# Tails of four heads in one product, two more transposes by DMA, and two MoE pieces begun on half their tokens

## Chip, core and metric

The kernel runs on one core of a Trainium2 chip. Its time is the device time of one execution in microseconds (us), and a kernel's time is the median over several executions.

## The reference

A forgetting attention, whose output is the input of a two-layer MoE block with a SiLU gate (one expert, no routing). 8 batches, 8 heads, 576 positions, head size 64; 4608 tokens of width 512, inner width 2048.

```python
scores = scale * np.matmul(q, k.transpose(0, 1, 3, 2))
cum = np.cumsum(np.log(np.clip(f, 0.0001, 1.0)), axis=-1)
scores = np.where(causal, -1e9, scores + cum[..., :, None] - cum[..., None, :])
attn = softmax(scores)
x = np.matmul(attn, v).transpose(0, 2, 1, 3).reshape(B * S, H * D)
h = x @ w_in
out = (h * (1.0 / (1.0 + np.exp(-h)))) @ w_out
```

The row part of the decay cancels in the softmax; the column part, exp(-cum), is multiplied into v and into a 65th column of ones beside it, so that one product gives both the weighted sum and its divisor.

## The kernel before

The order of the instructions of every engine is the order in which the Python code emits them. Three streams are woven together by hand: loads and conversions (queues of SP and POOL), attention, and MoE pieces that `fill` (through `slot`) emits between steps of the attention so that TensorE (PE) never has to stand.

**Positions.** 576 positions of a sequence are cut into a head of 128 (block 0), a rest of 384 and a tail of 64. All heads of the sequence blocks 0 are computed first, batch by batch (`turn0`, `scores0`, `out0`, `back0`): scores, exp on ScalarE (ACT), product with v, division on VectorE (DVE), and a transpose on PE whose copy (L391, ACT or DVE) writes the MoE input `x`. The first MoE group holds the heads of batches 0 to 3, 512 tokens; batches 4 and 5, then 6 and 7 follow as groups of 256.

**Rest and tails.** The main loop (`for m in range(NQ)`, 16 rounds) takes two units n = 2m and 2m + 1; a unit is two heads of a batch, and a batch is four units. `prepare` casts q and k for unit n + 2 on POOL (L400, L404), has SP transpose them by DMA (L428, `qkT`), and has SP load q, k for unit n + 4 (L158), the tails (L168) and v (L179); POOL multiplies v by its weights (L414). All of SP's transfers stand in one queue in the emitted order, and so do POOL's casts, multiplies and output stores (L592). `scores` makes the scores in three chunks (L460), their exp (L464, and L476 for the tails' `ut`), and DVE masks them (L469, and L483 for `ut`). `attend` multiplies by v into the PSUM tile `dn` (L507: 18 matmuls of 65 columns), and the tails of the unit's two heads follow into a seventh column group of the same tile (L516: 10 matmuls of 65 columns). There the left operand is 128 wide: 64 positions of one head beside 64 zeros, so that two heads accumulate into the two halves of the partitions. The zeros stand in the middle of `ut`, which has three parts (head, zeros, head); POOL writes them once with four memsets (L735). DVE then takes the reciprocal of the 65th column (L524) and multiplies (L525) into `xr`.

**Back.** `back(m - 1)` is emitted in round m, between the scores of the two units and ahead of the second `prepare`. For rounds with `BY_DMA[m]` (m from 4 to 14) SP transposes `xr` into `x` (L539) and the tails into `xt` (L543) by DMA; for the others PE transposes it in 7 matmuls (L549) and DVE copies it in two instructions (L552, L555). Each round has four `slot`s. A rest group becomes `ready` for MoE with the end of the next slot after its second `back`, and one slot later where that goes by DMA.

**MoE.** `m1_chunk(g, fc)` makes one of 16 pieces of the inner width for group g: 4 matmuls (L568) into a PSUM tile `hp`, tanh on ACT (L576) and the gate on DVE (L577), which writes `gt`. `m2_part` makes a quarter of the second layer for 128 tokens (L613, tile `po`, 4 matmuls); ACT copies the sum (L623) and POOL stores it (L592). `step` chooses between the two and goes on with whichever layer lags.

**Buffers.** The PSUM pool `pbig` has four buffers for `hp`, `po`, `dn`, `tx` and the rest; `sc` has two of its own (`psc`). A tile's buffer comes free when its last reader has finished, for `hp` the gate on DVE, for `dn` the multiply L525. `after` (L200) is a small transfer at the head of SP's main-loop loads that waits until half of w_out has landed.

Of the kernel before, what the change touches and what calls it, by code (L numbers as in the profile page):

```python
# [12 lines left out]
P = 128  # L13
# [5 lines left out]
def kernel(  # L19
# [62 lines left out]
    kT0 = [const.tile([P, NP, P], BF16, name=f"kT0_{b}") for b in range(B)]  # L82
    v0 = [const.tile([P, H, D + 1], BF16, name=f"v0_{b}") for b in range(B)]
    vps = [const.tile([P, NM, H, D + 1], BF16, name=f"vp_{i}") for i in range(2)]
    uts = [const.tile([P, NM + 1, 3, ST], BF16, name=f"ut_{i}") for i in range(4)]
    vfs = [const.tile([P, H, D + 1], FP32, name=f"vf_{i}") for i in range(4)]


# [356 lines left out]
    def scores(n, c):  # L445
        b, p = divmod(n, NP)
        if c == 0:
            us[n] = upool.tile([P, 2, UW], BF16, name="u", tag="u")
        u, ut = us[n], uts[n % 4]
        t = qkT[n]  # L450
        sc = psc.tile([P, 2, SM], FP32, name="sc", tag="sc")
        for kb, q0, q1, o in CHUNKS[c]:
            for i in range(2):
                r = slice(i * D, (i + 1) * D)
                if kb == 0:
                    kt = kT0[b][r, p, :]
                else:
                    k0 = RB if kb == NM else kb * P + RB
                    kt = t[r, k0 : k0 + P]
                nc.tensor.matmul(  # L460
                    sc[:, i, o : o + q1 - q0], lhsT=kt, rhs=t[r, q0:q1], start=True, stop=True
                )
        w = SM if c < 2 else T0
        nc.scalar.activation(  # L464
            out=u[:, :, c * SM : c * SM + w], in_=sc[:, :, 0:w], func=ACT.Exp, scale=scale
        )
        if c == 0:
            x = u[:, :, 0:RB].rearrange("p i (a t) -> p i a t", t=P)
            nc.vector.tensor_tensor(  # L469
                out=x,  # L470
                in0=x,
                in1=tri[:, None, None, :].to_broadcast([P, 2, NR, P]),
                op=ALU.mult,
            )
        if c == 2:
            nc.scalar.activation(  # L476
                out=ut[:, :, 0:3:2, :].rearrange("p k i t -> p i k t"),
                in_=sc[:, :, T0 : T0 + (NM + 1) * ST].rearrange("p i (k t) -> p i k t", t=ST),
                func=ACT.Exp,
                scale=scale,  # L480
            )
            x = ut[:, NM, 0:3:2, :]
            nc.vector.tensor_tensor(  # L483
                out=x, in0=x, in1=trit[:, None, :].to_broadcast([P, 2, ST]), op=ALU.mult
            )

    NGR = 2 * NR + 1

    BY_DMA = [2 * 2 <= m < NQ - 1 for m in range(NQ)]

    def attend(n):
        b, p = divmod(n, NP)
        if p % 2 == 0:
            xqs[n // 2] = xqp.tile([P, NGR, 2, D], BF16, name="xr", tag="xr", bufs=3)
        xq = xqs[n // 2]
        u, ut = us.pop(n), uts[n % 4]
        dn = pbig.tile([P, NGR, D + 1], FP32, name="dn", tag="big")

        def vals(kb, i):
            h = head(p, i)  # L500
            return v0[b][:, h, :] if kb == 0 else vbf[b][:, kb - 1, h, :]

        for i in range(2):
            for c in range(1, NM):
                for kb in range(c + 1):
                    o = AT[c, kb]
                    nc.tensor.matmul(  # L507
                        dn[:, i * NR + c - 1, :],
                        lhsT=u[:, i, o : o + P],
                        rhs=vals(kb, i),  # L510
                        start=(kb == 0),
                        stop=(kb == c),
                    )
        for i in range(2):
            for kb in range(NM + 1):
                nc.tensor.matmul(  # L516
                    dn[:, NGR - 1, :],
                    lhsT=ut[:, kb, i : i + 2, :].rearrange("p i t -> p (i t)"),
                    rhs=vals(kb, i),
                    start=(i == 0 and kb == 0),  # L520
                    stop=(i == 1 and kb == NM),
                )
        rec = recp.tile([P, NGR], FP32, name="rec", tag="rec")
        nc.vector.reciprocal(out=rec[:, :], in_=dn[:, :, D])  # L524
        nc.vector.tensor_tensor(  # L525
            out=xq[:, :, p % 2, :],
            in0=dn[:, :, 0:D],
            in1=rec[:, :, None].to_broadcast([P, NGR, D]),
            op=ALU.mult,
        )  # L530

    def back(m):
        b, c0 = m // 2, m % 2 * 2
# [24 lines left out]

    gts: dict[int, bass.AP] = {}

    def m1_chunk(g, fc):
        w = GW[g]
        if fc == 0:
            gts[g] = gpool.tile([P, NFC, w], BF16, name="gt", tag="gt")
        gt = gts[g]
        hp = pbig.tile([P, w], FP32, name="hp", tag="big")
        for cc in range(NCC):
            nc.tensor.matmul(  # L568
                hp[:, :],
                lhsT=w_in_bf[:, cc, fc * P : (fc + 1) * P],  # L570
                rhs=xcols(g, cc),
                start=(cc == 0),
                stop=(cc == NCC - 1),
            )
        th = tpool.tile([P, w], BF16, name="th", tag="th")
        nc.scalar.activation(out=th[:, :], in_=hp[:, :], func=ACT.Tanh, scale=0.5)  # L576
        nc.vector.scalar_tensor_tensor(  # L577
            out=gt[:, fc, :],
            in0=th[:, :],
            scalar=1.0,  # L580
            in1=hp[:, :],
            op0=ALU.add,
            op1=ALU.mult,
        )
# [142 lines left out]
    back0(1, on_act)  # L727
    out0(3, 1)
    back0(2, on_act)
    back0(3, on_act, on_dve)  # L730
    ready.add(0)
    nc.gpsimd.memset(trit[0:ST, :], 0.0)
    make_upper_triangular(nc, trit[ST:P, :], val=1.0, diag=True)
    for t in uts:
        nc.gpsimd.memset(t[:, :, 1, :], 0.0)  # L735
    for t in vps:
        nc.gpsimd.memset(t[0:ST, NR, :, :], 0.0)
    load_w_out(0)
# [84 lines left out]
    def slot(us_, first=0):  # L823
        n = len(stores)
        fill(us_, first)
        store(n)
        for x in pending:
            x[0] -= 1
        while pending and pending[0][0] == 0:
            ready.update(pending.pop(0)[1])  # L830

    for m in range(NQ):
        n = 2 * m
        piece = 1.7 if m < 2 else 2.4
        scores(n, 0)
        scores(n, 1)
        prepare(n)
        slot(piece, 2)
        if m > 0:
            back(m - 1)  # L840
            if m % 2 == 0:
                b = m // 2 - 1
                pending.append([1 + BY_DMA[m - 1], [REST_OF[b]] + ([TAILS_OF[b][0]] if b == NM - 1 else [])])
        scores(n, 2)
        scores(n + 1, 0)
        prepare(n + 1)
        slot(piece, 2)
        scores(n + 1, 1)
        scores(n + 1, 2)
        slot(piece, 2)  # L850
        attend(n)
        attend(n + 1)
        slot(min(3.5, max(0.8, behind() - LAG)) if m > 1 else 0.8, 1)
    back(NQ - 1)
    ready.update([REST_OF[B - 1], TAILS_OF[B - 1][0]])
# [36 lines left out]
```

The softmax here doesn't subtract the row's maximum and nothing guards it: scores larger than these inputs give would overflow.

## Time and profile before

| what | value |
|---|---|
| median of 6 runs | 347.32 us (345.23 to 348.28) |
| the profiled execution's own time | 348.45 us |
| its span, first to last instruction | 346.6 us |
| PE sc (L460) | 128-column matmuls x384, 64-column x256 and others |
| PE dn L507 / L516 | 576 / 320 matmuls of 65 columns |
| PE tx L549 | 35 matmuls, in 5 of 16 rounds |
| SP transposes | qkT x32, x x11, xt x11 |
| DVE L524 / L525 | 32 each, 203 / 624 ns |
| DVE L577, 384 columns | 128, 553 ns |
| ACT L576, 384 columns | 128, 504 ns |
| POOL memset of ut, L735 | 4, 1.28 us in all from 21.84 us |

A row of the groups gives engine, line, operation, the names and sizes of what is written and read, the number of instructions and their mean time. PE's durations overlap, because matmuls are pipelined: the time that one costs is the time from its start to the next one's start, so the text uses start-to-start times. A wait is put down to the engine and line that ended last before it. In the slices, a digit is a tenth of 8.67 us.

### The profile page before, as it was taken

Reading aid. Unit: us, or ns where it says so; the run is one execution under the profiler, and the core shown is the slowest. Engines: PE = TensorE matmul, PEld = TensorE weight load, DVE = VectorE, ACT = ScalarE, POOL = GpSimd, SP = SyncE. Lnnn points to the kernel's source line nnn. Section 1 sums busy time; section 2 is a strip of 40 time slices with the busy share of each in tenths; the row PEclk is TensorE's granted clock in tenths of the full one; section 3 lists DMA queues with packets and bytes.
Section 4 is the critical chain, followed back from the end, with each engine's and each line's share of the span. In section 5 each row is a group of like instructions: output and inputs, shape, how many; then the busy total and the mean of one; then the engine's idle time right before and its main releaser. Section 6 shows DMA issues by size and latency. Waiting matters only on the chain.

```text
span 346.6 us, 8892 instructions
## 1 busy us (share of the span) xinstructions
PE 335.8 (97%) x3567; PEld 199.2 (57%) x3567; DVE 185.8 (54%) x389; ACT 218.0 (63%) x401; POOL 129.2 (37%) x227
## 2 busy tenths in 40 slices
PE   8999999969998999999999999999999999999995
PEld 3654556647655566466565665656655565555654
DVE  4766645455668466457646654646645453535330
ACT  5866654866685857768759576685775934545341
POOL 8996224823518264236218126234420000010011
PEclk9999999999999999999999999999999999999999
DMA  8999989999689999899889989989832100010103
GB/s 154 197 185 220 200 160 150 220 210 185 164 177 208 187 201 158 170 210 167 154 193 187 159 154 220 158 191 188 170 91 56 35 32 30 32 46 32 46 36 87
DMA packets 141497, 50.44 MB, mean 146 GB/s; under 512 B 132368, under 2 KB 138768, under 8 KB 141456
## 3 DMA queue, kind: packets, MB, share of 16 engines
q1 hardware_dynamic: 131440, 32.70, 52.4%
q0 software_dynamic: 9856, 17.04, 21.1%
q8 instruction: 28, 0.46, 0.6%
q10 hardware_dynamic: 160, 0.13, 0.1%
q14 instruction: 13, 0.11, 0.1%
HBM read 36.85 MB, written 9.44 MB: 134 GB/s over the span
## 4 chain that ended last, share of the span: by engine, by line
PE 73%; DMA 11%; POOL 5%; SPq 4%; issue 3%; ACT 1%; DVE 1%; POOLq 0%
PE po L613 30%; PE hp L568 28%; PE sc L460 6%; PE dn L507 4%; DMA w_out_bf<-in_moe_w_out_dram 3%; DMA vf<-in_v_dram 3%; PE dn L516 2%; DMA qktf<-in_k_dram 2%; SPq L158 2%; DMA qf<-in_q_dram 2%; PE wm L232 1%; SPq L168 1%; DMA qkT<-qkb 1%; POOL v L341 1%; POOL w_in_bf L190 1%
## 5 line engine op out<-in xcount | busy, mean ns | idle before, releaser
L576 ACT ACTIVATE th<-hp 128x384 bf16<-128x384 f32 (+2 forms) x208 | 96.0, 478 | 90.9 <-PE hp L568 88.6
L577 DVE SCALAR_TENSOR_TENSOR gt<-th,hp 128x384 bf16<-128x384 bf16 (+2 forms) x208 | 106.0, 522 | 79.7 <-ACT th L576 76.1
L613 PE MATMUL po<-w_out_bf,gt 128*128 128x512 bf16 (+1 forms) x592 | 144.7, 374 | 0.0
L568 PE MATMUL hp<-x,w_in_bf 128*128 128x384 bf16 (+2 forms) x704 | 128.9, 322 | 0.2
L568 PEld LDWEIGHTS <-w_in_bf 128*128 128x128 bf16 x832 | 78.5, 98 | 55.2 <-issue 2.2
L464 ACT ACTIVATE u<-sc 128x1024 bf16<-128x1024 f32 (+1 forms) x96 | 75.2, 823 | 13.1 <-PE sc L460 13.0
L613 PEld LDWEIGHTS <-gt 128*128 128x128 bf16 x592 | 54.6, 98 | 49.7 <-issue 2.1
L592 POOL DMA_DIRECT2D out_dram<-osb x38 | 21.0, 552 | 130.2 <-ACT osb L623 83.0
L414 POOL TENSOR_TENSOR vp<-vf,w_bf 128x520 bf16<-128x520 f32 (+1 forms) x32 | 34.0, 1065 | 32.0 <-DMA vf<-in_v_dram 24.1
L469 DVE TENSOR_TENSOR u<-u,tri 128x768 bf16<-128x768 bf16 x32 | 22.2, 693 | 20.2 <-ACT u L464 20.1
L400 POOL CAST qkb<-qf 128x384 bf16<-128x384 f32 x32 | 17.6, 551 | 36.2 <-DMA qf<-in_q_dram 35.8
L483 DVE TENSOR_TENSOR ut<-ut,trit 128x128 bf16<-128x128 bf16 x32 | 12.0, 376 | 34.8 <-ACT ut L476 34.8
L623 ACT ACTIVATE osb<-po 128x512 f32<-128x512 f32 (+1 forms) x37 | 22.0, 596 | 12.4 <-PE po L613 12.3
L460 PE MATMUL sc<-qkT 64*128 64x128 bf16 (+1 forms) x640 | 26.5, 207 | 3.1 <-DMA qkT<-qkb 3.1
L460 PEld LDWEIGHTS <-qkT 64*128 64x128 bf16 x640 | 18.2, 95 | 14.1 <-issue 9.1
L476 ACT ACTIVATE ut<-sc 128x640 bf16<-128x640 f32 x32 | 23.4, 730 | 0.0
L507 PEld LDWEIGHTS <-u 128*128 128x128 bf16 x576 | 20.7, 98 | 4.1 <-issue 1.8
L507 PE MATMUL dn<-vp,u 128*128 128x65 bf16 x384 | 21.8, 194 | 0.0
L507 PE MATMUL dn<-v,u 128*128 128x65 bf16 x192 | 19.8, 194 | 1.6 <-DVE gt L577 1.6
L525 DVE TENSOR_TENSOR xr<-dn,rec 128x448 bf16<-128x448 f32 x32 | 20.0, 624 | 1.1
L400 POOL CAST qkb<-kf 128x384 bf16<-128x384 f32 x32 | 17.4, 542 | 6.5 <-DMA kf<-in_k_dram 6.5
L568 PE MATMUL hp<-xt,w_in_bf 128*128 128x256 bf16 x128 | 18.2, 273 | 0.3 <-DVE gt L577 0.2
(68 smaller groups left out, 205.3 us busy)
## 6 DMA issues: line engine op xcount, KB each, us to landing
out_dram<-osb POOLq DMA_DIRECT2D x32, 256.0 KB, 3.1
vf<-in_v_dram SPq DMA_DIRECT2D x26, 256.0 KB, 5.1
qf<-in_q_dram SPq DMA_DIRECT2D x64, 96.0 KB, 2.9
kf<-in_k_dram SPq DMA_DIRECT2D x64, 96.0 KB, 2.8
w_in_bf<-in_moe_w_in_dram POOLq DMA_DIRECT2D x4, 512.0 KB, 6.9
w_out_bf<-in_moe_w_out_dram POOLq DMA_DIRECT2D x4, 512.0 KB, 9.6
vf<-in_v_dram POOLq DMA_DIRECT2D x6, 256.0 KB, 10.2
qkb<-in_q_dram POOLq DMA_DIRECT2D x8, 128.0 KB, 5.2
```

Source lines behind the costliest of these rows:

```text
L400: nc.gpsimd.tensor_copy(out=t2[:, c0 : c0 + NR, :].rearrange("p c x -> p (c x)"), in_=t[:, :, :, :].rearrange("p c h d -> p (c h d)"),)
L414: nc.gpsimd.tensor_tensor(out=vbf[b][r, c, :, :], in0=vst[b][c][r, :, :], in1=w_bf[r, c + 1, b * H : (b + 1) * H, None].to_broadcast([n, H ...
L460: nc.tensor.matmul(sc[:, i, o : o + q1 - q0], lhsT=kt, rhs=t[r, q0:q1], start=True, stop=True)
L464: nc.scalar.activation(out=u[:, :, c * SM : c * SM + w], in_=sc[:, :, 0:w], func=ACT.Exp, scale=scale)
L469: nc.vector.tensor_tensor(out=x, in0=x, in1=tri[:, None, None, :].to_broadcast([P, 2, NR, P]), op=ALU.mult,)
L476: nc.scalar.activation(out=ut[:, :, 0:3:2, :].rearrange("p k i t -> p i k t"), in_=sc[:, :, T0 : T0 + (NM + 1) * ST].rearrange("p i (k t) ...
L507: nc.tensor.matmul(dn[:, i * NR + c - 1, :], lhsT=u[:, i, o : o + P], rhs=vals(kb, i), start=(kb == 0), stop=(kb == c),)
L568: nc.tensor.matmul(hp[:, :], lhsT=w_in_bf[:, cc, fc * P : (fc + 1) * P], rhs=xcols(g, cc), start=(cc == 0), stop=(cc == NCC - 1),)
L576: nc.scalar.activation(out=th[:, :], in_=hp[:, :], func=ACT.Tanh, scale=0.5)
L577: nc.vector.scalar_tensor_tensor(out=gt[:, fc, :], in0=th[:, :], scalar=1.0, in1=hp[:, :], op0=ALU.add, op1=ALU.mult,)
L613: nc.tensor.matmul(po[:, :], lhsT=gt[:, fc, tb * P : (tb + 1) * P], rhs=w_out_bf[:, fc, m0:m1], start=(fc == 0), stop=(fc == NFC - 1),)
L623: nc.scalar.activation(out=osb[:, :], in_=po[:, :], func=ACT.Copy, scale=0.5)
```

## The change

Four edits stand in the diff. `ut` loses its zeros: it has two parts, and the four memsets go. `attend` leaves the tails out; a new `attend_tails(m)` is emitted once per round after both units' `attend`, takes a PSUM tile `dt` from `pbig`, and multiplies the tails of two heads (128 columns, no zeros) by the values of both heads at once (130 columns): 10 matmuls for a round instead of 20, of whose result half is used. DVE takes one reciprocal and two multiplies of 64 partitions for it. `BY_DMA` begins at m = 2 instead of 4, which also makes batch 1's rest group ready one slot later, so that in round 4 two products of the second layer change places with two pieces of the first on the two sides of the attention. And `m1_begin` makes the first 256 columns (batches 0 and 1) of the first two MoE pieces, one ahead of the fourth batch's transposes and one behind them; `m1_chunk` then makes the other 256 columns of these two. SP, POOL and ACT otherwise keep their order (on ACT one tanh moves behind a copy in round 4).

```diff
@@ -82,7 +82,7 @@
     kT0 = [const.tile([P, NP, P], BF16, name=f"kT0_{b}") for b in range(B)]
     v0 = [const.tile([P, H, D + 1], BF16, name=f"v0_{b}") for b in range(B)]
     vps = [const.tile([P, NM, H, D + 1], BF16, name=f"vp_{i}") for i in range(2)]
-    uts = [const.tile([P, NM + 1, 3, ST], BF16, name=f"ut_{i}") for i in range(4)]
+    uts = [const.tile([P, NM + 1, 2, ST], BF16, name=f"ut_{i}") for i in range(4)]
     vfs = [const.tile([P, H, D + 1], FP32, name=f"vf_{i}") for i in range(4)]
 
 
@@ -474,27 +474,27 @@
             )
         if c == 2:
             nc.scalar.activation(
-                out=ut[:, :, 0:3:2, :].rearrange("p k i t -> p i k t"),
+                out=ut[:, :, :, :].rearrange("p k i t -> p i k t"),
                 in_=sc[:, :, T0 : T0 + (NM + 1) * ST].rearrange("p i (k t) -> p i k t", t=ST),
                 func=ACT.Exp,
                 scale=scale,
             )
-            x = ut[:, NM, 0:3:2, :]
+            x = ut[:, NM, :, :]
             nc.vector.tensor_tensor(
                 out=x, in0=x, in1=trit[:, None, :].to_broadcast([P, 2, ST]), op=ALU.mult
             )
 
     NGR = 2 * NR + 1
 
-    BY_DMA = [2 * 2 <= m < NQ - 1 for m in range(NQ)]
+    BY_DMA = [2 <= m < NQ - 1 for m in range(NQ)]
 
     def attend(n):
         b, p = divmod(n, NP)
         if p % 2 == 0:
             xqs[n // 2] = xqp.tile([P, NGR, 2, D], BF16, name="xr", tag="xr", bufs=3)
         xq = xqs[n // 2]
-        u, ut = us.pop(n), uts[n % 4]
-        dn = pbig.tile([P, NGR, D + 1], FP32, name="dn", tag="big")
+        u = us.pop(n)
+        dn = pbig.tile([P, 2 * NR, D + 1], FP32, name="dn", tag="big")
 
         def vals(kb, i):
             h = head(p, i)
@@ -511,23 +511,42 @@
                         start=(kb == 0),
                         stop=(kb == c),
                     )
-        for i in range(2):
-            for kb in range(NM + 1):
-                nc.tensor.matmul(
-                    dn[:, NGR - 1, :],
-                    lhsT=ut[:, kb, i : i + 2, :].rearrange("p i t -> p (i t)"),
-                    rhs=vals(kb, i),
-                    start=(i == 0 and kb == 0),
-                    stop=(i == 1 and kb == NM),
-                )
-        rec = recp.tile([P, NGR], FP32, name="rec", tag="rec")
+        rec = recp.tile([P, 2 * NR], FP32, name="rec", tag="rec")
         nc.vector.reciprocal(out=rec[:, :], in_=dn[:, :, D])
         nc.vector.tensor_tensor(
-            out=xq[:, :, p % 2, :],
+            out=xq[:, 0 : 2 * NR, p % 2, :],
             in0=dn[:, :, 0:D],
-            in1=rec[:, :, None].to_broadcast([P, NGR, D]),
+            in1=rec[:, :, None].to_broadcast([P, 2 * NR, D]),
             op=ALU.mult,
         )
+
+    def attend_tails(m):
+
+
+        b, h0 = m // 2, m % 2 * 4
+        xq = xqs[m]
+        dt = pbig.tile([P, 2, 2, D + 1], FP32, name="dt", tag="big")
+        for w in range(2):
+            ut = uts[(2 * m + w) % 4]
+            for kb in range(NM + 1):
+                vals = v0[b] if kb == 0 else vbf[b][:, kb - 1, :, :]
+                nc.tensor.matmul(
+                    dt[:, w, :, :],
+                    lhsT=ut[:, kb, :, :].rearrange("p i t -> p (i t)"),
+                    rhs=vals[:, h0 + w : h0 + 4 : 2, :],
+                    start=(kb == 0),
+                    stop=(kb == NM),
+                )
+        rec = recp.tile([P, 2, 2], FP32, name="rect", tag="rect")
+        nc.vector.reciprocal(out=rec[:, :, :], in_=dt[:, :, :, D])
+        for i in range(2):
+            r = slice(i * ST, (i + 1) * ST)
+            nc.vector.tensor_tensor(
+                out=xq[r, 2 * NR, :, :],
+                in0=dt[r, :, i, 0:D],
+                in1=rec[r, :, i, None].to_broadcast([ST, 2, D]),
+                op=ALU.mult,
+            )
 
     def back(m):
         b, c0 = m // 2, m % 2 * 2
@@ -558,17 +577,36 @@
 
     gts: dict[int, bass.AP] = {}
 
+    begun: dict[int, bass.AP] = {}
+
+    def m1_begin(fc):
+
+        w = GW[0] // 2
+        hp = pbig.tile([P, GW[0]], FP32, name="hp", tag="big")
+        for cc in range(NCC):
+            nc.tensor.matmul(
+                hp[:, 0:w],
+                lhsT=w_in_bf[:, cc, fc * P : (fc + 1) * P],
+                rhs=xg(0)[:, cc, 0:w],
+                start=(cc == 0),
+                stop=(cc == NCC - 1),
+            )
+        begun[fc] = hp
+
     def m1_chunk(g, fc):
         w = GW[g]
         if fc == 0:
             gts[g] = gpool.tile([P, NFC, w], BF16, name="gt", tag="gt")
         gt = gts[g]
-        hp = pbig.tile([P, w], FP32, name="hp", tag="big")
+        if g == 0 and fc in begun:
+            hp, c0 = begun.pop(fc), w // 2
+        else:
+            hp, c0 = pbig.tile([P, w], FP32, name="hp", tag="big"), 0
         for cc in range(NCC):
             nc.tensor.matmul(
-                hp[:, :],
+                hp[:, c0:w],
                 lhsT=w_in_bf[:, cc, fc * P : (fc + 1) * P],
-                rhs=xcols(g, cc),
+                rhs=xcols(g, cc) if c0 == 0 else xg(g)[:, cc, c0:w],
                 start=(cc == 0),
                 stop=(cc == NCC - 1),
             )
@@ -727,12 +765,12 @@
     back0(1, on_act)
     out0(3, 1)
     back0(2, on_act)
+    m1_begin(0)
     back0(3, on_act, on_dve)
+    m1_begin(1)
     ready.add(0)
     nc.gpsimd.memset(trit[0:ST, :], 0.0)
     make_upper_triangular(nc, trit[ST:P, :], val=1.0, diag=True)
-    for t in uts:
-        nc.gpsimd.memset(t[:, :, 1, :], 0.0)
     for t in vps:
         nc.gpsimd.memset(t[0:ST, NR, :, :], 0.0)
     load_w_out(0)
@@ -850,6 +888,7 @@
         slot(piece, 2)
         attend(n)
         attend(n + 1)
+        attend_tails(m)
         slot(min(3.5, max(0.8, behind() - LAG)) if m > 1 else 0.8, 1)
     back(NQ - 1)
     ready.update([REST_OF[B - 1], TAILS_OF[B - 1][0]])
```

## The prediction

> **What bounds the kernel now.** I read the page first.
>
> ```profile
> span 346.6 us, 8892 instructions
> ...
> PE 335.8 (97%) x3567; PEld 199.2 (57%) x3567; DVE 185.8 (54%) x389; ACT 218.0 (63%) x401; POOL 129.2 (37%) x227
> ...
> PEclk9999999999999999999999999999999999999999
> DMA  8999989999689999899889989989832100010103
> ```
>
> TensorE is busy 97% of the span at an undiminished clock, so its time is the sum of its instructions' start-to-start times plus its few waits. The DMA engines are as full until slice 28 (about 250 us). The waits of PE (in total, times, longest) say where these two meet:
>
> ```profile
> PE sc L460 <- DMA qkT<-qkb: 3.1, 2, 2.6
> PE dn L507 <- DVE gt L577: 1.6, 1, 1.6
> ```
>
> Then the chain that ended last, in order of time (start, us, what), in the stretch of the first of these waits:
>
> ```profile
> 75.09 1.22 SPq L428
> ...
> 78.60 4.68 DMA vf<-in_v_dram
> 83.28 3.77 DMA qkT<-qkb
> 87.04 0.05 issue
> 87.09 0.40 PE sc L460 x8
> 87.49 1.41 PE hp L568 x12
> ```
>
> Up to 87.09 us the chain runs through SP's queue and its loads, and PE stands waiting twice (2.6 us before 75.97, 0.4 before 87.09) for transposed q and k. From 87 us on the chain is PE. So **what PE saves before 87 us is waited away**, and what it saves or loses after it counts. I number units n (two heads) and pairs of units m as the code does; 87.09 is the scores of unit 5.
>
> **Begun pieces.** They issue 8 matmuls of 256 columns ahead and 8 in place of 8 of 512. Rows: 256 columns 109 ns start to start, 512 columns 216, so the columns cost the same. They fill holes: between the third and fourth batches' transposes PE stands from 16.62 to 17.09, then 17.21 to 17.42 and 17.54 to 17.84, 0.98 us. ScalarE's copy of batch 1 ends at 16.81; piece 0 runs 16.86 to 17.30, the fourth batch's transposes go 0.2 late, piece 1 runs 17.53 to 17.97, the second halves 18.03 to 18.90. The third piece starts at 18.90 instead of 17.84 + 8 x 0.216 = 19.57: 0.67 us ahead. In the built program the fifth piece is still the first to need a buffer back (the first piece's). Worth at the end: **0**, since the 2.6 us wait for unit 3's qkT takes it.
>
> **Zeros no longer written.** Four memsets of POOL (1.28 us at 21.84) go ahead of the w_out loads, which gate SP's first load at 36.1. The DMA engines have a backlog there (busy in every us from 22 to 48), so I take 0; bounds 0 and -1.28.
>
> **Transposes of pairs 2 and 3 by DMA.** PE loses 14 transposes at 56 ns start to start: **-0.78 us**. Four copies of DVE (551 and 214 ns, twice) go. SP gets two pairs of transposes at 1.21 + 1.23 = 2.44 us of issue. The first stands between unit 11's loads (end 107.12) and unit 9's transpose:
>
> ```profile
> 106.10 1.02 SPq L158 DMA_DIRECT2D kf<-in_k_dram  x2
> 108.03 1.22 SPq L428 DMA_TRANSPOSE qkT<-qkb  x1
> 109.30 1.13 SPq L158 DMA_DIRECT2D qf<-in_q_dram  x2
> ```
>
> SP idles 0.9 us here and 0.3 before the next transpose, so its lag becomes 4.9 - 1.2 = 3.7 us. After such a pair in the trace the next qkT landed 5.5 to 7.5 us after the pair's issue (nine of ten), median 6.4: unit 9 at 113.6 (114.6 at most), needed at about 115.2. The second pair issues at about 118.2 (was: unit 11 at 117.28, plus 2.44 less what is absorbed) and its first part lands 2.7 to 4.9 later, 121.0 to 123.2. It is a new wait: the first MoE piece after pair 4's attention reads it, with its third matmul, at about 122.9; behind it stand all of PE's pieces. I take 0.2 us for both; bounds 0 and 2.6 (1.4 at pair 4, 1.2 at pair 6, if PE runs early or the lag stays).
>
> **Tails in a product of their own.** Start to start a 65-column matmul is 30 ns; 130 columns have no row. Bounds are 30 and 109 (256 columns); the nearest row, 128 columns, has 56, so I take 57. Per pair PE goes from two groups of 28 (2 x 0.85 = 1.70) to 18 + 18 + 10: 0.54 + 0.54 + 0.57 = 1.65, a gain of 0.05. But a third buffer is taken from `pbig`'s four before MoE goes on, and DVE, which frees them, gets more to do: 0.20 + 0.56, twice, then 0.17 + 0.29 + 0.29, where it had 0.20 + 0.62, twice. (The 0.29, 64x128 results, has no row: bounds 0.21, a 128x128 copy, and 0.42, 256 elements; 0.29 continues the line through 448 elements, 624 ns, and 256, 423.) The built program's waits name the partner of each: the tails wait for the gate (gt) of the last piece ahead of the attention, the next three pieces for the multiplies of dn, dn and dt. Pair 5 shows the sizes; its attention began at 135.87:
>
> ```profile
> 135.94 1.21 DVE L577 SCALAR_TENSOR_TENSOR gt<-th,hp 128x384 bf16<-128x384 bf16 x2 [0.19 <-ACT th L576]
> 137.06 0.20 DVE L524 RECIPROCAL rec<-dn 128x7 f32<-128x7 f32 x1
> 137.29 0.62 DVE L525 TENSOR_TENSOR xr<-dn,rec 128x448 bf16<-128x448 f32 x1
> ```
>
> The last gate ends 1.28 us after the attention's start, because matmul, tanh and gate are a latency. PE is there at 1.08. So (0.05 from an end to PE, as at 87.04): tails 1.33 to 1.90; piece 1 waits for the first multiply, 1.98 (2.05 in the trace, less 0.07 for 64 elements fewer) + 0.05, and runs 2.03 to 2.68; piece 2 for the second, 2.83 to 3.48; piece 3 for the tails', 3.63 to 4.28. Before, three pieces (from 1.70, 0.65 each) ended at 3.66: **+0.62**. The same walk with each pair's own gate and order: pair 2 +0.48, 3 +0.07, 4 +0.18, 6 +0.18, 8 +0.18, 11 +0.19, 12 +0.03, 14 +0.32, and -0.07 to -0.05 for 7, 9, 10, 13, 15, where a po product or a free DVE covers. Sum from pair 2 on **+1.92 us** (pairs 0 and 1 lie before 87). Bounds: -1.0 (0.07 gained 14 times) and +8.7 (0.62 everywhere).
>
> **The wait at 107.7.** The mask of ut is held up there:
>
> ```profile
> 106.95 2.16 DVE L483 TENSOR_TENSOR ut<-ut,trit 128x128 bf16<-128x128 bf16 x1 [0.64 <-ACT ut L476]
> ```
>
> Its median is 0.23. POOL runs without a break from 106.82 to 110.15 and DVE gets through at 109.05; PE waits 1.7. In the change PE arrives there 0.48 later (pair 2) and 0.39 earlier (transposes), so the mask falls into the same run and the wait stays. Bounds: 0 and -1.74. If it goes, pair 3 costs 0.33 instead of 0.07 and the DMA waits are nearer.
>
> The Trainium skill (SBUF — State Buffer, Who interferes with whom) says that a VectorE instruction with two SBUF inputs and a GpSimd instruction that reads SBUF exclude each other, the first holding the ports for its whole instruction. By that the mask would have gone on when POOL's cast ended at 107.34; the row shows it held through three casts and a multiply. By the rule the wait would shrink under its slack at the least shift and the sum would end near -0.1 us; by the row it stays.
>
> **Sum**: -0.78 + 1.92 + 0.2 = **+1.3 us** on the profiled execution (348.45, span 346.6 and 1.8 around it), so 349.7 there. That execution lies 1.1 above the median of the six runs, 347.32; on the median 1.3 gives **348.6**. A difference of 0.5% (1.74 us: below 345.58, above 349.06) is about what a measurement of this kernel can tell from no change.
>
> **Rivals.**
> - *Slower: the DMA transposes become the bound* (chance 0.36 with larger buffer waits). For: DMA and SP hardly idle between 108 and 165, the second pair lands up to 123.2 where 122.9 is wanted. Against: units 10 to 12 have 8 us and more between landing and use. It decides where PE reaches the first piece after pair 4 before the transpose has landed. Price 2.6 in place of 0.2: +3.7, 351.0.
> - *Faster: DVE keeps ahead of PE at the attention* (0.20). It decides where the last gate ends before PE has passed dn and dn, as at pairs 7, 9, 13 and 15; with the mask through before POOL's run at 106.82 (a shift of 0.15 is enough) and the buffer waits at 0: -0.78 + 0 + 0.2 - 1.74 = -2.3, 345.0. Against: the gate's 1.28 is a latency that no idle engine shortens, and pair 2's waits push the mask the other way.
> - *It doesn't do what it says*: the begun pieces' 0.67 us survives nowhere. That is in my forecast; if it did survive, -0.67, 347.9, still within it.
>
> **How the numbers follow.** Forecast 0.44 (its own range 347.4 to 349.0), slower 0.36, faster 0.20: so the same within 0.5% 0.44, slower 0.36, faster 0.20. The range reaches into both rivals: 344.8 (the faster one and a little) to 352.0 (the slower one and 1 us more of buffer waits).
>
> **What would show it.** PE's waits: sc for qkT before 87 longer than 3.1 us by some 0.5, and unit 5's scores still at 87; new waits of dt for gt, and of hp for xr, 2 to 3 us in all; the tails ten matmuls at 57 ns; SP's unit 9 transpose near 109.7; the mask L483 above 1 us again near 107. I am wrong if unit 5's scores start a microsecond away from 87.09, if PE shows no waits after the tails, or if it waits over 1 us for a transposed x.

## The result and the profile after

| kernel | median | executions | ratio to before |
|---|---|---|---|
| before | 347.06 us (344.94 to 349.53) | 37 | |
| changed | 349.31 us (347.38 to 352.84) | 18 | 1.0063 [1.0042, 1.0084] |
| changed, a second time | 350.57 us (349.53 to 355.04) | 6 (before: 347.19, 20) | 1.0094 [1.0067, 1.0120] |

The change costs 2.2 us (1.5 to 2.9), and 3.3 us (2.3 to 4.2) in the second measurement. The comparisons leave out executions more than 1.5% above their kernel's fastest, which matters for f1 and g4 below, where 3 and 5 of 12 are left out (their medians over all executions are given too), and for e1 and g1, whose profiled execution is the one left out.

The two profiled executions do not show the loss as a difference of spans: before's (348.45 us) lies 1.4 us above the median of its 37 executions, the changed kernel's (348.34 us) 1.0 us below that of its 18. So the text compares stages and not spans. In the changed kernel's numbering L587 is the begun pieces, L606, L614 and L615 the pieces, their tanh and their gate (L568, L576, L577 before), L533 the tails' product, L515 and L516 as well as L541 and L544 the reciprocals and multiplies of `dn` and `dt`, L651 the second layer (L613), and L558 and L562 the DMA transposes (L539, L543). The page after:

```profile
span 346.5 us, 8625 instructions
...
PE 336.2 (97%) x3401; PEld 198.2 (57%) x3401; DVE 188.4 (54%) x433; ACT 218.0 (63%) x401; POOL 127.7 (37%) x223
...
PEclk9999999999999999999999999999999999999999
DMA  8999998999699879799799779799962100010113
```

TensorE is as full as before. Its waits (in total, times, longest):

```profile
PE sc L460 <- DMA qkT<-qkb: 2.0, 2, 1.3
PE wm L232 <- DVE warm L204: 1.2, 1, 1.2
PE hp L587 <- DMA w_in_bf<-in_moe_w_in_dram: 1.2, 1, 1.2
PE tp L286 <- DMA qkb<-in_k_dram: 0.4, 1, 0.4
PE dn L507 <- DVE gt L615: 0.3, 1, 0.3
```

The wait for `gt` at 107.7 us has gone from 1.6 to 0.3, a begun piece (L587) waits for `w_in`, and the longest wait for `qkT` (1.3) has another place: 112.4 us, unit 9. The chain that ended last (start, us, what) tells most. Before, it was PE from 87 us on. Now:

```profile
88.71 0.90 POOL qkb L400 x2
94.15 1.26 SPq L428
99.15 5.81 DMA vf<-in_v_dram
105.87 0.96 POOL qkb L400 x2
107.06 1.01 POOL vp L414
108.15 1.05 POOL vp L414
109.29 4.41 DMA qkT<-qkb
114.14 2.70 PE po L651 x12
117.43 0.69 issue
118.78 3.32 DMA x<-xr
122.15 3.12 PE hp L606 x18
```

The reader is to see that loads, POOL, SP's queue and the DMA carry the chain up to unit 9's `qkT`, that PE and ACT follow for 5 us, and that the transposed x of pair 3 comes last, to 122.15 us. **The bound that ended at 87 us before now ends at 122 us.** SP's queue has no gap over 0.15 us between 104 and 126 us, where before it had one of 0.92 and one of 0.28:

```profile
106.56 1.35 SPq L558 DMA_TRANSPOSE x<-xr  x1
108.01 1.18 SPq L562 DMA_TRANSPOSE xt<-xr  x1
109.29 1.24 SPq L428 DMA_TRANSPOSE qkT<-qkb  x1
...
118.78 1.28 SPq L558 DMA_TRANSPOSE x<-xr  x1
120.16 1.18 SPq L562 DMA_TRANSPOSE xt<-xr  x1
121.44 1.25 SPq L428 DMA_TRANSPOSE qkT<-qkb  x1
```

And DVE at pair 5's attention (columns: start, us, engine and line, operation), to be held against the three lines of before:

```profile
134.74 1.00 DVE L615 SCALAR_TENSOR_TENSOR gt<-th,hp 128x384 bf16<-128x384 bf16 x2
135.67 0.18 DVE L515 RECIPROCAL rec<-dn 128x6 f32<-128x6 f32 x1
135.89 0.56 DVE L516 TENSOR_TENSOR xr<-dn,rec 128x384 bf16<-128x384 f32 x1
136.36 0.19 DVE L515 RECIPROCAL rec<-dn 128x6 f32<-128x6 f32 x1
136.59 0.56 DVE L516 TENSOR_TENSOR xr<-dn,rec 128x384 bf16<-128x384 f32 x1
137.06 0.17 DVE L541 RECIPROCAL rect<-dt 128x4 f32<-128x4 f32 x1
137.26 0.59 DVE L544 TENSOR_TENSOR xr<-dt,rect 64x128 bf16<-64x128 f32 x2
```

From 87 us to the end, this profile is 1.32 us longer than before's (start of unit 5's scores to the end: 260.87 against 259.55). Cut at the starts of the units' scores:

| term, from unit 5's scores on | forecast | changed kernel's profile |
|---|---|---|
| 14 transposes fewer on PE (units 6 and 8) | -0.78 | -0.78 |
| the wait at 107.7 (unit 7) | 0 | -1.40 |
| tails and their buffer waits (units 5, 9 to 31) | +1.85 | +1.05 as the tails alone (f2) show it |
| unit 9's scores wait for `qkT` (unit 8) | } +0.2 | +1.48 |
| x of pair 3 (unit 9), and small ones at units 11, 15, 31 | } | +0.28, +0.7 |

(Pair 3's own tails, +0.07 in the forecast, lie in unit 7.) The sum came out as forecast by luck, from other terms, and only in this execution: the second profile of the same kernel shows +6.1 us over the same stretch, nearly all of it at the x of pair 3. The -1.40 and the +1.48 belong together. In the ten profiles with pair 2's transposes on DMA, PE waits either 1.0 us or more at 107.7 (seven of them) or for unit 9's `qkT` (three: the changed kernel, f4 and g2), and units 7 and 8 take 12.6 to 13.4 us together in all ten.

### The profile page after: what moved, and what is told of

Its sections match the earlier page's. It is cut to its first block, busy times and chain, and to the rows that moved or that the text cites. A ratio compares the mean times of both kernels' runs of the same rounds, so it can differ in the third digit from the quotient of the medians.

```text
span 346.5 us, 8625 instructions
## 1 busy us (share of the span) xinstructions
PE 336.2 (97%) x3401; PEld 198.2 (57%) x3401; DVE 188.4 (54%) x433; ACT 218.0 (63%) x401; POOL 127.7 (37%) x223
## 4 chain that ended last, share of the span: by engine, by line
PE 71%; DMA 9%; SPq 5%; ACT 4%; POOL 3%; DVE 3%; issue 3%; POOLq 0%; ACTq 0%
PE po L651 30%; PE hp L606 28%; PE sc L460 5%; PE dn L507 3%; SPq L158 3%; DMA vf<-in_v_dram 3%; DMA w_in_bf<-in_moe_w_in_dram 2%; ACT u L464 2%; PE dt L533 2%; DVE gt L615 2%; SPq L428 1%; DMA qkb<-in_k_dram 1%; PE tp L286 1%; DMA qkT<-qkb 1%; POOL qkb L400 1%
## 5 line engine op out<-in xcount | busy, mean ns | idle before, releaser
L614 ACT ACTIVATE th<-hp 128x384 bf16<-128x384 f32 (+2 forms) x208 | 95.9, 478 | 91.8 <-PE hp L606 85.4
L615 DVE SCALAR_TENSOR_TENSOR gt<-th,hp 128x384 bf16<-128x384 bf16 (+2 forms) x208 | 105.8, 522 | 76.7 <-ACT th L614 72.0
L651 PE MATMUL po<-w_out_bf,gt 128*128 128x512 bf16 (+1 forms) x592 | 144.4, 374 | 0.0
L606 PE MATMUL hp<-x,w_in_bf 128*128 128x384 bf16 (+2 forms) x704 | 128.1, 320 | 0.3
L606 PEld LDWEIGHTS <-w_in_bf 128*128 128x128 bf16 x832 | 78.0, 98 | 56.4 <-issue 2.5
L651 PEld LDWEIGHTS <-gt 128*128 128x128 bf16 x592 | 54.5, 98 | 49.8 <-issue 2.1
L414 POOL TENSOR_TENSOR vp<-vf,w_bf 128x520 bf16<-128x520 f32 (+1 forms) x32 | 35.1, 1098 | 46.7 <-DMA vf<-in_v_dram 27.5
L469 DVE TENSOR_TENSOR u<-u,tri 128x768 bf16<-128x768 bf16 x32 | 21.2, 663 | 18.9 <-ACT u L464 18.9
L483 DVE TENSOR_TENSOR ut<-ut,trit 128x128 bf16<-128x128 bf16 x32 | 10.3, 321 | 35.3 <-ACT ut L476 35.3
L507 PEld LDWEIGHTS <-u 128*128 128x128 bf16 x576 | 20.0, 97 | 3.4 <-issue 0.8
L507 PE MATMUL dn<-vp,u 128*128 128x65 bf16 x384 | 20.2, 193 | 0.0
L507 PE MATMUL dn<-v,u 128*128 128x65 bf16 x192 | 19.0, 193 | 0.5 <-DVE gt L615 0.3
L400 POOL CAST qkb<-kf 128x384 bf16<-128x384 f32 x32 | 16.4, 513 | 7.9 <-DMA kf<-in_k_dram 7.9
L606 PE MATMUL hp<-xt,w_in_bf 128*128 128x256 bf16 x128 | 18.2, 273 | 0.3 <-DVE gt L615 0.2
L516 DVE TENSOR_TENSOR xr<-dn,rec 128x384 bf16<-128x384 f32 x32 | 17.8, 558 | 1.1
```

The source lines that it names most:

```text
L400: nc.gpsimd.tensor_copy(out=t2[:, c0 : c0 + NR, :].rearrange("p c x -> p (c x)"), in_=t[:, :, :, :].rearrange("p c h d -> p (c h d)"),)
L414: nc.gpsimd.tensor_tensor(out=vbf[b][r, c, :, :], in0=vst[b][c][r, :, :], in1=w_bf[r, c + 1, b * H : (b + 1) * H, None].to_broadcast([n, H ...
L469: nc.vector.tensor_tensor(out=x, in0=x, in1=tri[:, None, None, :].to_broadcast([P, 2, NR, P]), op=ALU.mult,)
L507: nc.tensor.matmul(dn[:, i * NR + c - 1, :], lhsT=u[:, i, o : o + P], rhs=vals(kb, i), start=(kb == 0), stop=(kb == c),)
L606: nc.tensor.matmul(hp[:, c0:w], lhsT=w_in_bf[:, cc, fc * P : (fc + 1) * P], rhs=xcols(g, cc) if c0 == 0 else xg(g)[:, cc, c0:w], start=(cc ...
L615: nc.vector.scalar_tensor_tensor(out=gt[:, fc, :], in0=th[:, :], scalar=1.0, in1=hp[:, :], op0=ALU.add, op1=ALU.mult,)
```

## The experiments

Ratios are to the kernel before, with 95% intervals. Three series were run, each with its own runs of the kernel before. The theory at the start (A) was that the buffer waits of the tails' product are the loss.

**e1, no begun pieces.**

```diff
-    m1_begin(0)
-    m1_begin(1)
```

> The changed kernel without the two begun pieces (tails and transposes by DMA stay). Theory A (the third PSUM buffer that the tails take is the loss; the begun pieces are worth nothing at the end): as slow as the changed kernel, 1.5 to 2.9 us above before; in the profile no wait for w_in near 17 us and the fourth batch's transposes near 17.1. Rival B (the first begun piece waits for w_in and holds up what stands behind it, and that reaches the end): the loss falls by a microsecond or more, to under 1.2 us above before.

351.99 us, 1.0120 [1.0077, 1.0162]: not faster than the changed kernel, so rival B fell; the 4.2 us above before are more than theory A's 1.5 to 2.9 too. Its profile, of the longest of its six executions (355.36 us), waits 2.1 us for the x of pair 3, which before never came from a DMA.

**e2, pairs 2 and 3 transposed by PE again.**

```diff
-    BY_DMA = [2 <= m < NQ - 1 for m in range(NQ)]
+    BY_DMA = [2 * 2 <= m < NQ - 1 for m in range(NQ)]
```

> The changed kernel with the transposes of pairs 2 and 3 on TensorE again (tails and begun pieces stay). Theory A: the 0.78 us of TensorE comes back and the wait of unit 9's scores for its transposed q and k (1.3 us in the changed kernel's profile) goes, so 1.5 to 2.5 us above before. Rival C (the two added DMA transposes make the loss): under 0.7 us above before. Both: no wait of sc for qkT near 112 us.

348.48 us, 1.0024 [0.9998, 1.0050]. Most of the loss goes; the 0.8 us that is left lies just above rival C's 0.7 and below theory A's 1.5 to 2.5. From unit 5 on the profile is 0.4 us shorter than before's (259.14).

**e3, tails in `dn` again.** The code of before for `ut`, the zeros and `attend`, and no `attend_tails`.

> The changed kernel with the tails back in dn, with the zeros and their memsets (begun pieces and transposes by DMA stay). Theory A: the loss falls by 1.5 to 2, to between -0.3 and 0.9 us above before, and from unit 9's scores to unit 31's the profile takes 156.5 to 157.0 us, as before (156.7), where the changed kernel takes 158.2. Rivals B and C: still 1.5 us or more above before.

351.2 us, 1.0132 [1.0083, 1.0181]. Without the tails' product the loss is as large or larger, so theory A fell. The profile (350.25 us) shows this execution's loss ahead of unit 5, whose scores start at 89.11, behind a wait of 2.8 us for `qkT` near 74 us and 3.4 us at half clock; from unit 5 to the end it takes 259.28 us, 0.27 less than before.

**e4, the tails behind the slot.**

```diff
-        attend_tails(m)
         slot(min(3.5, max(0.8, behind() - LAG)) if m > 1 else 0.8, 1)
+        attend_tails(m)
```

> The changed kernel with the tails' product emitted behind the slot of MoE work that follows the attention, instead of ahead of it: the same instructions, and the third buffer is taken where pieces have freed others. Theory A: of the 1.5 us between unit 9's scores and unit 31's at least 1 goes (157.2 or less), and the time is 0.5 to 1.3 us above before. If the loss were the added work of VectorE or the wider matmuls themselves, it would stay at 158.2 and 1.5 to 2.9.

353.91 us, 1.0199 [1.0157, 1.0241]. PE reaches the first MoE piece after pair 4's attention at 120.71, and its third matmul needs the x of pair 3, which lands at 124.28:

```profile
120.71 0.49 PE L606 MATMUL hp<-x,w_in_bf 128*128 128x384 bf16 x2
124.32 4.76 PE L606 MATMUL hp<-x,w_in_bf 128*128 128x384 bf16 x18 [3.12 <-DMA x<-xr]
```

Two matmuls, then 3.12 us of nothing, then 18 matmuls. PE being early gains nothing there. But these 18 take 4.76 us where the changed kernel's 18 take 3.12 (its chain, 122.15). The windows of this kernel (stretch, length, busy us of PE, PEld, DVE, ACT, POOL, then PEclk, DMA share, GB/s) show why:

```profile
125.20:128.60 3.40, 3.40 (x13) 1.65 (x12) 1.67 (x3) 1.60 (x4) 0.00 (x0) 0.51 0.69 155
128.60:132.00 3.40, 3.40 (x36) 2.05 (x35) 2.56 (x6) 2.46 (x4) 1.48 (x2) 0.99 1.25 236
```

The granted clock was 0.51 for 3.4 us behind the wait.

The next four take one part of the change alone, or one pair of the transposes back. The theory now (A again in their texts): the two added DMA transposes are the loss.

**f1, before with `BY_DMA` from 2 alone.**

> The kernel before with one part of the change alone: the x of pairs 2 and 3 transposed by DMA. Theory A (the two added DMA transposes are the loss: the transpose of unit 9 is issued later and lands late, and the transposed x of pair 3 lands after PE has reached the first MoE piece that reads it): PE waits for unit 9's qkT (before, no wait there) and over 1 us for x at the first piece after pair 4's attention; 1.003 to 1.012 of the kernel before. Rival B (the tails' third buffer is the loss): 14 transposes fewer on PE, 0.998 to 1.000, and no wait for x over 0.5 us. Rival C (the loss is interaction, each part alone is harmless): within 0.002 of the kernel before.

348.41 us, 1.0000 [0.9972, 1.0027]; over all 12 executions the median is 0.2% above before's, and four of them, those with a mean granted clock of 0.995 or less, took 350.0 to 354.0 us, where the longest of before's 35 took 349.9. In the profile PE waits 0.64 us for the x of pair 3 (theory A said over 1) and not at all for unit 9's `qkT`; its two waits for `qkT` stand at units 3 and 5, as before. Alone the part is no loss that its median shows; a wait for the x is there.

**f2, before with the tails' product alone.**

> The kernel before with one part alone: the tails in a product of their own, without zeros. Theory A: the buffer waits behind the attention cost their 1.5 us from unit 9 on and are partly given back at the wait near 107 us; 1.000 to 1.005. Rival B: the tails carry the whole loss, 1.005 to 1.008. Rival C: within 0.002. In all of them the tails are ten matmuls at 57 to 62 ns and new waits of PE for xr and gt of 2 to 3 us are seen, and no wait for a transposed x.

348.19 us, 1.0024 [0.9998, 1.0051]. Unit 9 to unit 31 takes 157.40 us against 156.72: the buffer waits cost 0.68 there. The wait at 107.7 is 0.2.

**f3, before with the begun pieces alone.**

> The kernel before with one part alone: the first two MoE pieces begun with half of their columns. All theories: the begun piece waits about 1 us for the first quarter of w_in, the fourth batch's transposes go 0.5 to 1.2 us later, and what is lost or gained is absorbed by the wait for unit 3's qkT; 0.998 to 1.003. Against them: if a wait of the fourth batch's chain is carried on past unit 5's scores (87.09 us before), 1.003 or more.

347.59 us, 0.9992 [0.9968, 1.0015]: nothing. Its begun piece waits 0.2 us for `w_in`, not about 1. From unit 5 on, its profile is like before's (259.37 and 259.55).

**f4, the changed kernel with pair 3 by PE.**

```diff
-    BY_DMA = [2 <= m < NQ - 1 for m in range(NQ)]
+    BY_DMA = [m == 2 or 4 <= m < NQ - 1 for m in range(NQ)]
```

> The changed kernel, with pair 3's x transposed by PE again and pair 2's left on DMA. Theory A in its two halves: the wait of unit 9's scores for qkT comes from pair 2's transpose and stays (about 1.3 us), the wait for pair 3's x is gone in every execution; so between the kernel with both on PE (1.0024) and the changed kernel (1.0063): 1.003 to 1.005. If the late x of pair 3 is the whole loss: 1.002 or less. If pair 2's transpose is the whole: 1.006. Rival B: no change against the changed kernel apart from 7 transposes (0.4 us): 1.006 to 1.008.

348.55 us, 1.0020 [0.9994, 1.0047], as with both pairs on PE. The interval hardly meets those of the changed kernel, so most of its loss goes with pair 3's transpose. This edit also makes batch 1's rest group ready a slot earlier, as e2's does, which changes the order of MoE pieces in round 4; the two are not told apart by it. The parts alone sum to 1.0000 + 0.0024 - 0.0008 = 1.0016, against the 1.0063 of all three. That points to an interaction but does not show one: each of these ratios is known to about 0.0025, and f1's 1.0000 is without its three longest executions (the mean of all 12 is 0.44% above before's).

The last four ask whether the place of the two transposes in SP's queue is the cause.

**g1, the changed kernel again.**

> The changed kernel once more, beside the next three on the same chip. Theory A (the two added DMA transposes stand in SP's queue at the wrong places: pair 2's x ahead of unit 9's q and k, pair 3's x behind unit 10's) and its rival B (the tails) both expect 1.004 to 1.0085 again; its profile shows the wait for unit 9's qkT and, in this one or not, one for the x of pair 3, as far as that lands behind PE's third matmul.

350.57 us, 1.0094 [1.0067, 1.0120]. The profile shows no wait for unit 9's `qkT`, which both theories expected. But this time the profiled execution (355.04 us, the longest of its six) fell on the late x of pair 3. Its first wait and its DMA and PEclk slices:

```profile
PE hp L606 <- DMA x<-xr: 3.1, 1, 3.1
```

```profile
PEclk9999999999999969999999999999999999999999
DMA  8999998999699899888979769979832300000103
```

```profile
122.95 0.49 PE L606 MATMUL hp<-x,w_in_bf 128*128 128x384 bf16 x2
126.55 5.92 PE L606 MATMUL hp<-x,w_in_bf 128*128 128x384 bf16 x18 [3.12 <-DMA x<-xr]
```

The same two matmuls and the same hole as in e4, in the changed kernel itself; the 6 in the PEclk row, at 124 to 132 us, is 6.8 us at half clock behind it, and the 18 matmuls take 5.92. SP issued that x at 120.98, 2.2 us later than in the first profile, and it landed 5.5 us later, at 126.51, where the first took 3.3.

**g2, pair 3's transposes early.** TensorE's order is unchanged.

```diff
         scores(n, 1)
+        if m == 4:
+            back(3)
         prepare(n)
         slot(piece, 2)
         if m > 0:
-            back(m - 1)
+            if m not in (0, 4):
+                back(m - 1)
```

> The changed kernel with the two DMA transposes of pair 3 issued ahead of unit 10's transposes and unit 12's loads; TensorE's order is untouched. Theory A: x of pair 3 lands 4 us or more before PE wants it, no execution waits for it; the wait for unit 9's qkT stays (pair 2's transpose is still ahead of it). 1.002 to 1.005, and less spread. If the late x of pair 3 has no part in the loss: as the changed kernel, 1.006.

350.42 us, 1.0104 [1.0070, 1.0137]. The x of pair 3 lands at 118.1, 5 us ahead of its use, and is not waited for; the loss stays. So that one wait is not the cause by itself.

**g3, and pair 2's late.** As g2, and `back(2)` moved behind `prepare(7)`.

> As the one before, and pair 2's two DMA transposes moved behind unit 9's transposes and unit 11's loads. Theory A: unit 9's qkT lands near 110, 3 us or more ahead of its use, and its scores wait no longer; units 8 to 10 take 14.6 us as before the change, and what is left is the buffer waits (1.5 us from unit 9 on) less 0.8 of transposes and up to 1.7 of the wait near 107: 0.999 to 1.003. Rival B: 1.005 or more still.

351.29 us, 1.0093 [1.0055, 1.0131]. From unit 8's scores to unit 10's it takes 14.22 us, less than before's 14.61: both waits are gone, as expected, and the loss stays. A wait has moved on to pair 7, a small one in this execution (349.30 us, 2 us below the kernel's median):

```profile
178.07 0.48 PE L606 MATMUL hp<-x,w_in_bf 128*128 128x384 bf16 x2
179.22 0.97 PE L606 MATMUL hp<-x,w_in_bf 128*128 128x384 bf16 x5 [0.66 <-DMA x<-xr]
```

The figure two, hole, rest is the one at pair 3, two batches later (pair 5's reader comes at 150 us, pair 7's at 178).

**g4, tails in `dn` again and the transposes moved.** e3 with the edits of g3.

> The kernel of tails in dn again, with zeros (1.0132 with the two transposes where the change has them), and the two DMA transposes moved as in the kernel before this. Theory A: both waits gone, no buffer waits added, 14 transposes fewer on PE: 0.995 to 1.000, faster than both kernels. If it stays at 1.008 or more, that kernel's loss was not these transposes but something ahead of them (its wait of 2.9 us near 74 us and the clock after it), and theory A does not explain it.

351.63 us, 1.0064 [1.0027, 1.0101]; over all 12 executions the median is 1.3% above before's. Not faster than either kernel: the forecast of theory A failed here too. Its profile waits 0.40 us for the x of pair 5 and 2.08 for that of pair 7 (in its numbering L587 is the pieces):

```profile
179.89 0.49 PE L587 MATMUL hp<-x,w_in_bf 128*128 128x384 bf16 x2
182.45 1.30 PE L587 MATMUL hp<-x,w_in_bf 128*128 128x384 bf16 x7 [2.08 <-DMA x<-xr]
```

**What the series shows together.** For each kernel, when the x of an odd pair landed, minus when PE's third matmul behind the next attention was due (0.16 us after the second); positive is late. Then the last transposed x whose landing stands in the chain that ended last, and the profile's time from unit 5's scores to the end:

| kernel | pair 3 | pair 5 | pair 7 | last x in the chain, us | unit 5 to the end, us | ratio |
|---|---|---|---|---|---|---|
| before | (PE) | -3.4 | -4.6 | none | 259.55 | 1 |
| f3 begun pieces alone | (PE) | -4.3 | -5.6 | none | 259.37 | 0.9992 |
| f2 tails alone | (PE) | -4.8 | -3.7 | none | 259.17 | 1.0024 |
| e2 pairs 2, 3 on PE | (PE) | -3.7 | -3.5 | none | 259.14 | 1.0024 |
| f4 pair 3 on PE | (PE) | -2.0 | -0.5 | none | 259.83 | 1.0020 |
| f1 DMA alone | +0.8 | -0.7 | -0.1 | 123.2 | 260.09 | 1.0000 |
| changed | +0.2 | 0.0 | -0.4 | 122.1 | 260.87 | 1.0063 |
| g1 changed again | +3.2 | -4.9 | -5.0 | 126.5 | 265.67 | 1.0094 |
| e1 | +2.2 | -0.9 | +0.4 | 185.3 | 264.24 | 1.0120 |
| e3 | +0.3 | +0.5 | -1.2 | 152.3 | 259.28 | 1.0132 |
| e4 | +3.2 | -2.7 | -4.8 | 124.3 | 265.07 | 1.0199 |
| g2 | -5.2 | +0.2 | +0.2 | 179.6 | 260.65 | 1.0104 |
| g3 | -4.7 | -0.2 | +0.8 | 179.2 | 260.79 | 1.0093 |
| g4 | -6.0 | +0.5 | +2.2 | 182.4 | 262.00 | 1.0064 |

With two more pairs on SP's queue, the 3 to 5 us that the x of pairs 5 and 7 had in hand are gone, whichever transposes are moved; only executions that have already stood 3 us for pair 3 (g1, e4) have 2.7 us or more in hand again. The chains agree. In all nine profiles with pair 3's x on DMA the path runs through the landing of a transposed x at 122 us or later; in the five with it on PE no transposed x stands in the chain, and from 87.1 us on nothing of SP's queue or the DMA. In f1, whose median shows no loss, it reads:

```profile
119.23 3.98 DMA x<-xr
123.20 0.04 issue
123.24 3.11 PE hp L568 x18
```

So the theory that is left (A2): SP's queue and the DMA fall behind by the two pairs of transposes, do not catch up until about 180 us, and one of the reads of a transposed x between 122 and 185 us stands or only just does not, which one being a matter of the execution. It explains why moving them helped nothing and why taking one pair away did. That the path runs there is shown by the nine chains; that this is the whole loss is not. The theory was formed after the last run, and a kernel that keeps pairs 2 and 3 on DMA and puts pairs 4 and 5 on PE would test it and was not run. The profiles of e3, g2 and g3 show at most 1.3 us of it from unit 5 on, where their medians lose 3 to 4, and e3's loss lies ahead of unit 5. The order of the MoE pieces in round 4, which changes with pair 3's transposes, was not tested by itself.

## Why the prediction was right or wrong

The range held the time and the sign was the forecast's, but the likeliest case, within 0.5%, did not come: 1.0063 [1.0042, 1.0084] lies beyond it, with an interval that reaches back over its edge, and the second measurement lies clear of it. That the forecast (+1.3 us on the profiled execution) met that profile is luck, as the table of terms shows.

- **What bounds the kernel: half right.** PE's own time decides after 87 us only as long as the loads keep ahead; the changed kernel's chain shows them ahead no longer, up to 122 us. The forecast's own mark, unit 5's scores within a microsecond of 87.09, failed (85.66 in the profile). The 14 profiles have this start between 85.25 and 89.33 with no order by kernel, so what the change does before 87 us stays open.
- **Begun pieces: 0 right, its reason wrong.** "Piece 0 runs 16.86 to 17.30" failed. The first quarter of `w_in` landed at 17.78, and PE waited:

```profile
16.24 0.40 PE L390 MATMUL tx<-ident_bf,xq 128*128 128x128 bf16 x4
17.82 0.61 PE L587 MATMUL hp<-x,w_in_bf 128*128 128x256 bf16 x4 [1.18 <-DMA w_in_bf<-in_moe_w_in_dram]
18.27 0.39 PE L390 MATMUL tx<-ident_bf,xq 128*128 128x128 bf16 x4
```

  The fourth batch's transposes, behind the piece, went at 18.27 instead of 17.09. The working looked at the copy that the piece reads and not at the weights, which land at about the time when the MoE could begin anyway (16.83 before). In e2, e3, f3, g1, g2 and g3 this wait is 0.2 to 0.4 us. Alone, the part is worth nothing (f3).
- **Zeros no longer written: 0**, not tested by itself.
- **Tails: the mechanism right, the size about double.** The tails are ten matmuls at about 60 ns (in pair 5's attention 135.88 to 136.50, and 57 were forecast), and PE's weight loads for `hp` now wait 1.9 us for `xr` (L516 1.2, L544 0.7), as listed. But from unit 9 to unit 31 the product costs 0.68 (f2) and 0.67 (e2) where the pairs 4 to 14 were summed to 1.5. Pair 5 measured +0.45 for +0.62, pair 14 +0.33 for +0.32, pair 2 +0.38 for +0.48; the +0.18 of pairs 4, 6 and 8 were 0.0.
- **The wait at 107.7: failed.** It "falls into the same run and the wait stays": it is 0 to 0.3 us in five of the nine profiles with the tails' product and 1.2 us or more in all in the other four, and 1.0 or more in all five without. The forecast moved only PE. POOL's run moves too, because it follows a multiply of v (L414) that waits for v's load, and a store: the casts began 4.87 us after unit 7's scores before, 5.36 in the changed kernel and 3.53 in f2, with the mask at 5.0 in all three. A race of two streams was priced as if one stood still; that was worth 1.4 us, and where pair 2's transposes go by DMA the next wait, unit 9's, took it back.
- **DMA transposes: the step that decided, mis-sized.** "I take 0.2 us for both" failed; the profile has 1.5 us at unit 9 and 0.3 at the x of pair 3, the second profile 6.1 at the latter. At unit 9 the DMA's side was forecast well and PE's was not: `qkT` landed at 113.70 (113.6 forecast), but PE was there at 112.43 instead of 115.2, 1.4 us early by unit 5 and 1.4 by the wait at 107.7. For the x of pair 3 the landing was forecast at 121.0 to 123.2 and measured at 122.1, 123.2, 124.3, 124.6, 126.5 and 127.6 us in six profiles, and the use, forecast at 122.9, came at 121.0 to 125.4. The rival *DMA transposes become the bound* named place and mechanism, and gave 351.0; what was missing in its price is the half clock behind the wait (2.8 us in g1: unit 9 took 17.27 us instead of 11.17, of which the third matmul's delay is 3.28), and in the "against" the look at pairs 5 and 7. Their margins, 3.4 and 4.6 us, stood in the trace of before, and 4.9 us of queue were being added ahead of them.
- **"It doesn't do what it says"** was right as to the begun pieces' time.

## What to carry to other kernels

Here, with the queue and the DMA engines busy throughout, transposes moved from TensorE to DMA took the margin of later transfers in that queue. So list the margin of each later use (landing to first reader) and compare the smallest with what is added, instead of asking where the added one itself lands. If a wait comes and goes between executions, price it as a race with both sides moving; and compare medians and stages, since one profile of each kernel here showed equal spans for a 2 us loss. None of the three parts alone shows a loss clear of the noise, and none of the versions run beat the kernel before by a measurable amount.

## What the runs showed of the hardware

**Behind a short wait TensorE's clock may fall to half for 3.4 us.** A granted clock of 0.5 was recorded for 3.4 or 6.8 us behind waits of 2.1 (e1), 2.8 (e3), 3.1 (e4, g1) and 2.5 us (f3), and in e1 also behind several short ones between 15.4 and 18.4 us; behind waits of 2.6 (before), 2.3 (g2), 2.2 and 2.1 us (g4) it was not. In e1 the two stretches began at 18.55 and 127.77 us, 109.2 us apart. The Trainium skill (TensorE: Matmul & The Clock Gate, Part 1: The HAM clock gate) says that the activity window is free-running, 3413 ns long, and that the clock falls after an idle window; 109.2 is 32.0 such windows, so the trace agrees on the grid, while the waits that sufficed here are all shorter than one. That a wait can fall anywhere on such a grid fits that one of 2.5 us cost the clock in f3 and one of 2.6 did not in before. It also shows in the times: the changed kernel's 13 executions with a mean granted clock above 0.9965 have a median of 348.77 us, the other five 351.42; for before, in the second series, 347.67 (17) and 347.85 (18). In before, a fall seems to cost next to nothing. Where it lies in before no profile shows; in f3, which differs by the begun pieces alone, it lies at 75.6 to 79.0 us, in the stretch where loads and not PE carry the chain of before.

**A mask of DVE that started during POOL's run got through only between POOL's two multiplies.** In four profiles the mask (L483, two inputs from SBUF) was held during POOL's casts and ended within 0.1 us of the end of the first multiply behind them (start plus half of the pair's length): f2 108.07 and 108.02, g3 108.48 and 108.43, g1 109.17 and 109.13, f3 109.71 and 109.66. The wait's end is POOL's, so its length shrinks by as much as the mask comes later: 0.82 us in f2, which started 0.32 into the multiply, 2.03 in f3. The casts leave no gap: in `before` they start at 106.82, 107.26 and 107.72 and take 0.52, 0.51 and 0.29 us, the first multiply starts at 107.98, and the first gap of POOL (0.08 us in all these profiles) is the one between the multiplies. In f4 and g2 the mask started 0.5 and 0.2 us ahead of the first cast and took 0.23 and 0.32 us. The rule that the prediction weighed (the Trainium skill, SBUF — State Buffer, Who interferes with whom) is an exclusive lock of the shared ports, and these rows do not contradict it; what failed is the prediction's reading that the mask would go on at the end of a single cast.
